# Half-height matmul pairs throughout: a spectral filter and a gated feed-forward block on one core

## The chip, the cores and the metric

The kernel runs on one core of one Trainium2 chip. The metric is the device time of one execution in microseconds. The profiles shown come from one execution that the hardware profiler recorded; their times are microseconds from the start of the span unless marked ns. PE is the matrix engine (its weight loads are PEld), DVE the vector engine, ACT the scalar engine, POOL the general engine, SP the queue that issues most DMAs.

## The reference

```python
xn = _layernorm(x, axis=-1)                       # x: 1 x 2048 x 448
y  = irfft2(rfft2(xn) * (w_r + 1j * w_i), s=(2048, 448))
gate, up = xn @ W_gate, xn @ W_up                 # 448 x 1792 each
h  = relu(gate) * up
out = x + y + h @ W_down                          # 1792 x 448
```

All in float32. The kernel works in pairs of float16 numbers, a high part and the rest, so that one product of float32 numbers becomes three float16 products: high by high, high by low, low by high.

## The kernel before, in words

The 2048 rows stand as 16 blocks `n2` of 128 rows. Four column chunks `q` hold four blocks each: 512 rows of x, transposed into `Tq[q]`, with the 448 features on the partitions. The 1792 hidden features are 14 tiles `f` of 128, in three groups of 5, 5 and 4.

**Units.** A gate-and-up unit is one tile `f` and one chunk `q`. It fills one `gu` tile of two PSUM banks, one for gate (`g` = 0) and one for up (`g` = 1); there are two such tiles. Since 448 is three times 128 and 64 more, a bank takes ten full matmuls of 128 rows by 512 columns (`SEQ`, line 905 in the profile) and one of 64 rows (`TOP`, line 912). The 64-row ones of two units are put together by `gu_halves`: four stand in a row, two for a unit and two for its mate, the next unit, which they open. Two of them, on the upper and the lower 64 rows of the array and in two banks, form a pair. A unit is then read by ACT (`gu_relu`, line 940), DVE (`gu_times`, line 944), ACT (`gu_hi`, line 948) and DVE (`gu_lo`, line 952), which leave `h` as high and low part. The `gu` tile is free after line 944.

**Down blocks.** A block of 128 rows takes `3 * len(group)` matmuls of 128 by 448 into one `dn` bank of two (`dn_mm`, line 976). ACT seeds the bank with the running sum (`dn_seed`, line 969) and takes it out again (`dn_post`, line 980). Four blocks of a chunk follow each other after the second unit at the latest that comes behind the chunk's last unit. The last four are written out by hand at the end (`dn_end`, line 1008).

**The transforms.** The spectral part runs as background work in a list `bg`, item by item, between the units. Its products are `f_dft` (line 467) and `i_ddft` (line 801), 48 half-height matmuls of 58 or 56 columns each in alternation on the two halves, `f_sdft` (line 500), three full ones of 464 columns, and `i_sdft` (line 771), twelve full ones of 128 columns, each for one block. They use two `fx` banks. Their additions and rotations are on DVE.

**Order.** An opening is written out by hand (`OPENING`); it holds the first five units. Behind it, a scheduler lays each engine's instructions in order from a time line, by priority and by what is ready; the program gives the order of units, priorities, and a few edges (`issue_after`, `add_manual_dep`). How much background work goes to a unit is set by `took`, `PE_US` and `LASTGU`, the number of units at the end that get none.

Of the kernel before, what the change touches and what calls it, by code (L numbers as in the profile page):

```python
# [10 lines left out]
F32 = mybir.dt.float32  # L11
# [6 lines left out]
S, D, F = 2048, 448, 1792  # L18
NF = F // 128
KC = 29  # L20
NG = 8
GW = 2 * KC
XW = NG * GW
# [17 lines left out]
"""  # L41
EXPMASK = 0x7F800000
EXPONE = float(1 << 23)
LASTGU = 9
SQ = 2.0 ** -16


# [99 lines left out]
def tile_gfnet_reglu(ctx: ExitStack, tc: tile.TileContext, x, xr, wgu, wd, wf, ident, c_fd, c_fm, c_im, c_row, c_id,  # L147
                     out):
    nc = tc.nc
    V, A, P, G = nc.vector, nc.scalar, nc.tensor, nc.gpsimd  # L150
# [4 lines left out]
    def mt(shape, dt, name, bufs=1):  # L155
        return main.tile(shape, dt, name=name, bufs=bufs)
# [4 lines left out]
    def fx():  # L161
        return psum.tile([128, 512], F32, name="fx", bufs=2)
# [8 lines left out]
    Tq = {q: mt([128, 9, 512], F16, f"T{q}") for q in CHUNKS}  # L171
# [11 lines left out]

    eps = mt([128, 1], F32, "eps")
    V.memset(eps, 1e-5)

# [19 lines left out]
    state = {}  # L206
# [27 lines left out]
    wst, wdst, fm_t, im_t, wf_t = {}, {}, {}, {}, {}  # L234
# [133 lines left out]
    tp, side, last = {}, {}, {}  # L368
# [40 lines left out]
        copy(Tq[q][:, (3, 4, 8)[i], :], tp["end", i], act)  # L409


    Fq, Xh, yps, cur = {}, {}, {}, {}
    RT = float(np.sqrt(0.5))

# [28 lines left out]
    def chained(m, prev):  # L443
        if "opened" in state and prev is not None:
            tc.add_manual_dep(m, prev.name, NOSYNC, reason="half passes stand together")
        return m

    def two_banks():
# [43 lines left out]
    def f_lo(a, n2):  # L492
        V.tensor_tensor(Xh[n2][:, 1], f_part(a, n2), Xh[n2][:, 0], op=OP.subtract)

    def f_sdft(n2):
        y = fx()[:, 0:XW]
        yps[n2] = y.rearrange("p (g c k) -> p g c k", g=NG, c=2)
        m, xh = fm_t[n2], Xh[n2].rearrange("p a g k -> p a (g k)")
        for i, (a, b) in enumerate(((0, 0), (0, 1), (1, 0))):
            P.matmul(y, m[:, a, :], xh[:, b], start=(i == 0), stop=(i == 2), skip_group_check=True)  # L500

    def rotate(t, b, p, sgn):

# [124 lines left out]
    sps, pg, pgh, vt = {}, {}, {}, {}  # L628
# [136 lines left out]
    def i_sdft(n2):  # L765
        ps = fx()
        v, m = state["vt"][:, :, n2 // 8].rearrange("p a g k -> p a (g k)"), im_t[n2]
        for g in range(4):
            o = ps[:, 128 * g:128 * (g + 1)]
            for i, (h, c) in enumerate(((0, 0), (0, 1), (1, 0))):  # L770
                P.matmul(o, v[:, h, 128 * g:128 * (g + 1)], m[:, c, :], start=(g + i == 0), stop=(i == 2),  # L771
                         skip_group_check=True)
        sps[n2] = ps

    def i_pqhi(n2):
        pgh[n2] = it([128, 1024], F16, "wf", 6).rearrange("p (a k) -> p a k", a=2)
# [49 lines left out]
    wt, wdt, wsc = {}, {}, {}  # L826
# [67 lines left out]
    hps, ht = {}, {}  # L894

    SEQ = [(r + 4 * k, r) for r in range(3) for k in (0, 1)] + [(t, 5 + t) for t in range(3)] + [(3, 4)]
    TOP = ((slice(0, 64), 3), (slice(64, 128), 4))

    def gu_open(f, q):
        hps[f, q] = psum.tile([128, 2, 512], F32, name="gu", bufs=2)  # L900

    def gu_full(f, q, gs, cs, start, stop, seq=SEQ):
        for g in gs:
            for i, (a, b) in enumerate(seq):
                last["P"] = P.matmul(hps[f, q][:, g, cs], wt[f, g][:, a, :], Tq[q][:, b, cs],  # L905
                                     start=(start and i == 0), stop=(stop and i == len(seq) - 1)).ins
# [8 lines left out]
    NOSYNC = mybir.DependencyInfo(mybir.DependencyClass.NoSync, mybir.DependencyReason.DATA)  # L915
    opened = set()

    def gu_unit(f, q, mate):

        gs, cs = (0, 1), slice(0, 512)  # L920
        if (f, q) in opened:
            gu_full(f, q, gs, cs, False, True)
            return
        gu_open(f, q)
        gu_full(f, q, gs, cs, True, False)
        gu_halves(f, q, mate)
# [33 lines left out]
    dps = {}  # L960
# [4 lines left out]
    def dn_seed(g, n2):  # L965

        dps[n2] = dn_bank()
        seeded.add(n2)
        A.activation(dps[n2][:, 0:D], xy[n2], AF.Copy, scale=dinv[:, g:g + 1])  # L969

    def dn_mm(fs, n2):
        q, j = n2 % 4, n2 // 4
        js = slice(128 * j, 128 * (j + 1))
        for f in fs:
            for a, b in ((0, 0), (0, 1), (1, 0)):
                last["P"] = P.matmul(dps[n2][:, 0:D], ht[f, q][:, a, js], wdt[f][:, b, :], start=False,  # L976
                                     stop=(f == fs[-1] and a == 1), skip_group_check=True).ins

    def dn_post(g, n2):
        last["A"] = A.activation(xy[n2], dps[n2][:, 0:D], AF.Copy, scale=dsc[:, g:g + 1]).ins  # L980
        seeded.discard(n2)
        if n2 in late:
            late.discard(n2)
            i_acc(n2)
# [33 lines left out]

    bg = []
    marks = {}  # L1020
    PE_US = {"f_dft": 0.85, "f_sdft": 0.59, "i_sdft": 0.65, "i_ddft": 0.82, "row_dft": 0.2}

    def add(cost, fn, *a):
        bg.append((cost, PE_US.get(fn.__name__, 0.0), fn, a))

# [37 lines left out]
    for k, a in enumerate(seq):  # L1063
        add(1.99, f_a, a)
        add(2.14, f_b, a)
        for n2 in (a, a + 8):
            add(0.0, f_hi, a, n2)
        if k:
            for n2 in (seq[k - 1], seq[k - 1] + 8):
                add(1.09 * (n2 >= 8), f_y1, n2)  # L1070
        if k < 7:
            add(0.0, f_dft, seq[k + 1], seq[k + 1] + 8)
        for n2 in (a, a + 8):
            add(0.54, f_lo, a, n2)
            add(0.0, f_sdft, n2)
        for fn, q in extra.get(k, ()):
            fn(q)
    for n2 in (7, 15):
# [8 lines left out]
    def back(k0):  # L1087
        add(bf[0], inv1, k0)
        if k0 >= 4:
# [6 lines left out]
    rows = [lambda: (row_wf(), row_hi()), row_lo, lambda: row_dft(0), row_mul, row_hi2, row_lo2,  # L1096
            lambda: row_dft(1), row_ev]
# [30 lines left out]
    def both(c, fn, p):  # L1128
        for n2 in (p, p + 8):
            add(c, fn, n2)  # L1130
# [11 lines left out]
    for p in range(8):  # L1142
        if p:
            both(0.6, i_pqlo, p - 1)
            add(0.0, i_ddft, p - 1, p + 7)
        if p < 7:
            both(0.0, load_im, p + 1)
        add(2.14, i_mix, p, 1)
        add(0.0, i_hi, p)
        if p < 6:  # L1150
            bring(p + 2)
        add(1.1, i_lo, p)
        both(0.0, i_sdft, p)
# [34 lines left out]
    groups, f0 = [], 0  # L1188
# [176 lines left out]
    for i, u in list(enumerate(units))[len(groups[0]):]:  # L1365
        is_gu = u[0] == "gu"
        if is_gu:
            _, g, f, q = u
            run_bg(until=marks["T", q])
            gu_unit(f, q, (mates.get(u) or (0, 0, None, None))[2:])  # L1370
        elif i < len(units) - 4:
            _, g, n2, _ = u
            dn_mm(groups[g], n2)
            nxt = [v for v in units[i + 1:i + 3] if v[0] == "dn"][1:]
# [8 lines left out]
        if i >= len(units) - 4:  # L1383
            continue
        if is_gu:
            with tc.high_priority(offset=400):
                gu_post(f, q)
                if units[i + 1][0] == "dn" and i + 1 < len(units) - 4:
                    for v in units[i + 1:i + 3]:
                        dn_seed(v[1], v[2])  # L1390
        else:
            with tc.high_priority(offset=400):
                dn_post(g, n2)
                for v in nxt:
                    dn_seed(g, v[2])
            if g == len(groups) - 1:
                store(n2)
        anchors.append(last["V"])
        act_anchors.append(last["A"])
    run_bg(until=len(bg))  # L1400
    dn_end(len(groups) - 1, [u[2] for u in units[-4:]])


_ORDER = ["x", "xr", "wgu", "wd", "wf", "ident", "c_fd", "c_fm", "c_im", "c_row", "c_id"]
# [42 lines left out]
```

## Time and profile before

| | |
|---|---|
| Time, median of 2 runs | 440.02 us (439.99 to 440.05) |
| The profiled execution's own time | 440.03 us |
| Its span | 438.3 us |
| PE busy | 431.6 us, 98% |
| DVE busy | 372.7 us, 85% |
| ACT busy | 255.7 us, 58% |
| POOL busy | 37.6 us, 9% |
| DMA moved | 39.53 MB, mean 90 GB/s |

The page of the profile gives busy time by engine, the groups of instructions by line of the kernel with their mean length, and the chain of work that ended last. Matmuls are pipelined: the length of one reaches past the start of the next, so the rate of PE is read from the distance between starts in the timeline. A row of the timeline merges instructions of one line: start, time to the end of the last, engine, line, count, and in brackets the idle time ahead of it with what ended it.

### The profile page before, as it was taken

To read this page: it belongs to the slowest core of one execution; us is meant where nothing else is said; L and a number is where in the kernel's file an instruction comes from. 1 tells how busy PE (TensorE), PEld (TensorE's weight loads), DVE (VectorE), ACT (ScalarE), POOL (GpSimd) and SP (SyncE) were. 2 spreads that over 40 slices of the span, in tenths; PEclk is the share of its full clock that TensorE was granted. 3 is DMA by queue.
4 is the path that set the end of the run, shared out by engine and by line. 5 is a ranking of instruction groups with operands and counts; after the bars stand their busy time and mean duration, and the time that the engine had idled before them with its cause. 6 is when DMAs were issued, how large, how long until landed. Compare 5 with 4: busy or idle time off the path is not lost.

```text
span 438.3 us, 8110 instructions
## 1 busy us (share of the span) xinstructions
PE 431.6 (98%) x3014; PEld 209.5 (48%) x3014; DVE 372.7 (85%) x920; ACT 255.7 (58%) x516; POOL 37.6 (9%) x72
## 2 busy tenths in 40 slices
PE   7999999999999999999999999999999999999997
PEld 3644544454444444444444444444555555554544
DVE  6998798999977989899999999798999989867213
ACT  6897493686457855724513675564665754763630
POOL 1140040043400040000000011000000000000000
PEclk9999999999999999999999999999999999999999
DMA  7869992042000463531402100020111211301102
GB/s 258 265 164 320 339 256 64 2 68 43 3 1 0 145 190 113 165 126 35 134 8 85 44 1 1 2 84 3 55 57 45 73 61 33 119 30 43 51 35 84
DMA packets 37720, 39.53 MB, mean 90 GB/s; under 512 B 17952, under 2 KB 32576, under 8 KB 37680
## 3 DMA queue, kind: packets, MB, share of 16 engines
q1 hardware_dynamic: 37680, 39.01, 29.6%
q8 instruction: 23, 0.38, 0.4%
q14 instruction: 17, 0.14, 0.1%
HBM read 24.25 MB, written 3.67 MB: 64 GB/s over the span
## 4 chain that ended last, share of the span: by engine, by line
PE 97%; ACT 1%; DVE 1%; DMA 1%; issue 0%
PE gu L905 56%; PE dn L976 27%; PE gu L912 3%; PE fx L771 2%; PE fx L500 2%; PE fx L467 1%; PE fx L801 1%; PE dn L1008 1%; PE gu L1008 1%; DMA y<-in_xr 1%; ACT tt L330 1%; PE fx L406 0%; DVE bst L265 0%; PE fx L1008 0%; ACT junk L192 0%
## 5 line engine op out<-in xcount | busy, mean ns | idle before, releaser
L905 PE MATMUL gu<-T,wt 128*128 128x512 f16 (+1 forms) x1138 | 256.1, 376 | 0.0
L905 PEld LDWEIGHTS <-wt 128*128 128x128 f16 x1138 | 108.1, 98 | 130.3 <-issue 10.2
L976 PE MATMUL dn<-wdt,h 128*128 128x448 f16 x624 | 126.6, 353 | 0.0
L976 PEld LDWEIGHTS <-h 128*128 128x128 f16 x624 | 60.2, 98 | 57.4 <-issue 0.7
L948 ACT ACTIVATE h<-g 128x512 f16<-128x512 f32 x56 | 35.1, 627 | 67.4 <-DVE g L944 67.2
L944 DVE SCALAR_TENSOR_TENSOR g<-gu,g 128x512 f32<-128x512 f32 x56 | 38.4, 686 | 24.0 <-ACT g L940 23.8
L940 ACT ACTIVATE g<-gu 128x512 f32<-128x512 f32 x56 | 33.0, 589 | 36.3 <-PE gu L905 18.9
L952 DVE TENSOR_TENSOR h<-g,h 128x512 f16<-128x512 f32 x56 | 38.3, 686 | 7.0 <-ACT h L948 7.0
L980 ACT ACTIVATE xy<-dn,dsc 128x448 f32<-128x448 f32 x44 | 27.6, 628 | 28.4 <-PE dn L976 28.4
L195 POOL PARTITION_ALL_REDUCE wm<-wm x15 | 14.1, 947 | 170.4 <-ACT junk L192 170.4
L969 ACT ACTIVATE dn<-xy,dinv 128x448 f32<-128x448 f32 x44 | 27.7, 632 | 0.6
L858 DVE SCALAR_TENSOR_TENSOR wt<-wst,wsc,wt 128x512 f16<-128x512 f32 x28 | 20.4, 745 | 3.4 <-ACT wt L854 3.4
L854 ACT ACTIVATE wt<-wst,wsc 128x512 f16<-128x512 f32 x28 | 19.2, 714 | 1.0 <-DVE wsc L202 0.9
L192 ACT ACTIVATE junk<-wst 128x512 bf16<-128x512 f32 x28 | 17.4, 621 | 1.8 <-DMA wst<-in_wgu 1.5
L912 PE MATMUL gu<-T,wt 64*128 64x512 f16 x112 | 17.0, 382 | 0.0
L520 DVE TENSOR_TENSOR y<-y,y 128x464 f32<-128x464 f32 x21 | 13.4, 637 | 1.1 <-DMA row<-y 1.0
L780 DVE SCALAR_TENSOR_TENSOR wf<-fx,wf 128x512 f16<-128x512 f32 x16 | 10.5, 687 | 4.4 <-ACT wf L777 4.3
L265 DVE BATCH_NORM_STATS2 bst<-y 128x6 f32<-128x448 f32 x16 | 9.2, 620 | 5.1 <-DMA y<-in_xr 5.1
L521 DVE TENSOR_TENSOR y<-y,y 128x464 f32<-128x464 f32 x21 | 13.4, 636 | 0.0
L771 PEld LDWEIGHTS <-vt 128*128 128x128 f16 x192 | 11.5, 98 | 1.9
L771 PE MATMUL fx<-im,vt 128*128 128x128 f16 x192 | 12.2, 219 | 0.0
L807 ACT ACTIVATE xy<-fx,fsc 128x448 f32<-128x448 f32 x14 | 8.1, 630 | 6.9 <-PE fx L801 6.9
(162 smaller groups left out, 500.4 us busy)
## 6 DMA issues: line engine op xcount, KB each, us to landing
wst<-in_wgu SPq DMA_DIRECT2D x28, 256.0 KB
wf<-in_wf SPq DMA_DIRECT2D x16, 232.0 KB
sw<-y SPq DMA_DIRECT2D x32, 114.2 KB
sw<-wst SPq DMA_DIRECT2D x16, 228.4 KB
y<-in_xr SPq DMA_DIRECT2D x16, 224.0 KB
xy<-in_x SPq DMA_DIRECT2D x16, 224.0 KB
out<-xy SPq DMA_DIRECT2D x15, 224.0 KB
wdst<-in_wd SPq DMA_DIRECT2D x14, 224.0 KB
```

Of the source, the lines that this page charges most:

```text
L771: P.matmul(o, v[:, h, 128 * g:128 * (g + 1)], m[:, c, :], start=(g + i == 0), stop=(i == 2), skip_group_check=True)
L854: A.activation(w[:, 0:4, :], wst[f, g], AF.Copy, scale=wsc[f, g])
L858: V.scalar_tensor_tensor(w[:, 4:8, :], st, sc, w[:, 0:4, :], op0=OP.mult, op1=OP.subtract)
L905: last["P"] = P.matmul(hps[f, q][:, g, cs], wt[f, g][:, a, :], Tq[q][:, b, cs], start=(start and i == 0), stop=(stop and i == len(seq) - 1 ...
L912: m = P.matmul(hps[f, q][:, g, 0:512], wt[f, g][rows, 7, :], Tq[q][rows, b, :], start=start, stop=not start).ins
L940: last["A"] = A.activation(g1s[f, q], hps[f, q][:, 0, :], AF.Relu, scale=2.0 ** -22).ins
L944: last["V"] = V.scalar_tensor_tensor(g1, hps[f, q][:, 1, :], 2.0 ** -22, g1, op0=OP.mult, op1=OP.mult).ins
L948: A.activation(ht[f, q][:, 0, :], g1s[f, q], AF.Copy)
L952: V.tensor_tensor(h[:, 1, :], g1s.pop((f, q)), h[:, 0, :], op=OP.subtract)
L969: A.activation(dps[n2][:, 0:D], xy[n2], AF.Copy, scale=dinv[:, g:g + 1])
L976: last["P"] = P.matmul(dps[n2][:, 0:D], ht[f, q][:, a, js], wdt[f][:, b, :], start=False, stop=(f == fs[-1] and a == 1), skip_group_check= ...
L980: last["A"] = A.activation(xy[n2], dps[n2][:, 0:D], AF.Copy, scale=dsc[:, g:g + 1]).ins
```

## The change

All gate-and-up matmuls behind the opening, all down blocks but the last four, and the products `f_sdft` and `i_sdft` become half-height matmuls, issued in pairs. In a pair, one matmul works on the upper 64 rows of the array and writes one bank, the other works on the lower 64 rows and writes another bank. A first round gives each bank one half of the rows, a second round the other half with the sides swapped. The 64-row products of a unit form one more pair of that unit; mates remain in the opening only.

A bank must not be written from both halves at once. So the first matmul of the second round waits for a memset of one element, `tick`, on POOL, and that memset waits for the last matmul of the first round.

Down blocks are now units of two blocks, which fill both `dn` banks together. At most one such unit stands between two gate-and-up units, and the first comes behind the first unit of the next chunk. `f_sdft` and `i_sdft` take two blocks, and both `fx` banks, at a time. `LASTGU` goes from 9 to 7, and the costs that spread the background work follow the new sizes.

```diff
-LASTGU = 9
+LASTGU = 7
...
+    tick = mt([1, 1], F32, "tick")
...
+    SIDE = (slice(0, 64), slice(64, 128))
...
+    def ended(m):
+        with tc.high_priority(offset=4000):
+            r = G.memset(tick, 0.0).ins
+        tc.add_manual_dep(r, m.name, SYNC, reason="behind the rows' product")
+        return r
+
+    def beside(pair, start, stop, prev=None, skip=True):
+        m = None
+        for o, w, x in pair:
+            with tc.high_priority(offset=2000 if m else 0):
+                m = chained(P.matmul(o, w, x, start=start, stop=stop, skip_group_check=skip).ins, m)
+            if prev is not None:
+                tc.add_manual_dep(m, ended(prev).name, SYNC, reason="the other half of the rows has ended")
+                prev = None
+        last["P"] = m
+        return m
...
-    def f_sdft(n2):
+    def f_sdft(a, b):
...
+        for s in range(2):
+            for i, (c, d) in enumerate(((0, 0), (0, 1), (1, 0))):
+                r = beside([(y, m[SIDE[k != s], c, :], xh[SIDE[k != s], d]) for k, (y, m, xh) in enumerate(prods)],
+                       s + i == 0, s == 1 and i == 2, r if s and i == 0 else None)
...
-    def gu_unit(f, q, mate):
...
+    def gu_unit(f, q):
+        fresh = (f, q) not in opened
+        if fresh:
+            gu_open(f, q)
+        passes = [[(*TOP[g], 7) for g in range(2)]] if fresh else []
+        passes += [[(SIDE[g != s], b, a) for g in range(2)] for s in range(2) for a, b in SEQ]
+        for i, p in enumerate(passes):
+            m = beside([(hps[f, q][:, g, :], wt[f, g][rows, a, :], Tq[q][rows, b, :]) for g, (rows, b, a) in enumerate(p)],
+                   fresh and i == 0, i == len(passes) - 1, m if i == len(passes) - 10 else None, False)
...
-    def dn_mm(fs, n2):
+    def dn_mm(fs, ns):
...
+        for s in range(2):
+            for f in fs:
+                for a, b in ((0, 0), (0, 1), (1, 0)):
+                    r = beside([(dps[n2][:, 0:D], ht[f, q][SIDE[k != s], a, js[k]], wdt[f][SIDE[k != s], b, :])
+                            for k, n2 in enumerate(ns)], False, s == 1 and f == fs[-1] and a == 1,
+                           r if s and f == fs[0] and a + b == 0 else None)
...
-        if k % 2 and pend:
-            units += pend
-            pend = []
+        if pend and pend[0][2] % 4 != u[3]:
+            units.append(pend.pop(0))
         if u[2] == groups[u[1]][-1]:
-            pend = [("dn", u[1], u[3] + 4 * j, None) for j in range(4)]
+            pend += [("dn", u[1], u[3] + 8 * j, u[3] + 8 * j + 4) for j in range(2)]
...
-    took = lambda u: 4.55 if u[0] == "gu" else 0.56 * len(groups[u[1]])
+    took = lambda u: 4.55 if u[0] == "gu" else 1.12 * len(groups[u[1]])
```

More of the change, by code (lines that the diff above doesn't have):

```diff
@@ L493, in f_lo @@
         V.tensor_tensor(Xh[n2][:, 1], f_part(a, n2), Xh[n2][:, 0], op=OP.subtract)
-    def f_sdft(n2):
[L496 to L500, printed above, removed]
+    def f_sdft(a, b):
+        prods = []
+        for n2 in (a, b):
+            y = fx()[:, 0:XW]
+            yps[n2] = y.rearrange("p (g c k) -> p g c k", g=NG, c=2)
+            prods.append((y, fm_t[n2], Xh[n2].rearrange("p a g k -> p a (g k)")))
+        for s in range(2):
+            for i, (c, d) in enumerate(((0, 0), (0, 1), (1, 0))):
+                r = beside([(y, m[SIDE[k != s], c, :], xh[SIDE[k != s], d]) for k, (y, m, xh) in enumerate(prods)],
+                       s + i == 0, s == 1 and i == 2, r if s and i == 0 else None)
     def rotate(t, b, p, sgn):
@@ L763, in i_lo, with i_sdft @@
             V.scalar_tensor_tensor(lo[:, b], u[:, b], fsc[:, 0:1], hi[:, b], op0=OP.mult, op1=OP.subtract)
[L765 to L773, printed above, removed]
+    def i_sdft(a, b):
+        prods = []
+        for n2 in (a, b):
+            sps[n2] = fx()
+            prods.append((sps[n2], state["vt"][:, :, n2 // 8].rearrange("p a g k -> p a (g k)"), im_t[n2]))
+        for s in range(2):
+            for g in range(4):
+                o = slice(128 * g, 128 * (g + 1))
+                for i, (h, c) in enumerate(((0, 0), (0, 1), (1, 0))):
+                    r = beside([(ps[:, o], v[SIDE[k != s], h, o], m[SIDE[k != s], c, :])
+                            for k, (ps, v, m) in enumerate(prods)], s + g + i == 0, s == 1 and i == 2, r if s and g + i == 0 else None)
     def i_pqhi(n2):
@@ L969, in dn_seed @@
         A.activation(dps[n2][:, 0:D], xy[n2], AF.Copy, scale=dinv[:, g:g + 1])
-    def dn_mm(fs, n2):
[L972 to L977, printed above, removed]
+    def dn_mm(fs, ns):
+        q = ns[0] % 4
+        js = [slice(128 * (n2 // 4), 128 * (n2 // 4 + 1)) for n2 in ns]
+        for s in range(2):
+            for f in fs:
[3 more added lines that the diff above has]
+                           r if s and f == fs[0] and a + b == 0 else None)
     def dn_post(g, n2):
@@ L1020, in tile_gfnet_reglu @@
     marks = {}
-    PE_US = {"f_dft": 0.85, "f_sdft": 0.59, "i_sdft": 0.65, "i_ddft": 0.82, "row_dft": 0.2}
+    PE_US = {"f_dft": 0.85, "f_sdft": 1.18, "i_sdft": 1.3, "i_ddft": 0.82, "row_dft": 0.2}
     def add(cost, fn, *a):
@@ L1074, in tile_gfnet_reglu @@
             add(0.54, f_lo, a, n2)
-            add(0.0, f_sdft, n2)
+        add(0.0, f_sdft, a, a + 8)
         for fn, q in extra.get(k, ()):
@@ L1152, in tile_gfnet_reglu @@
         add(1.1, i_lo, p)
-        both(0.0, i_sdft, p)
+        add(0.0, i_sdft, p, p + 8)
         both(0.0, i_pqhi, p)
@@ L1369, in tile_gfnet_reglu @@
             run_bg(until=marks["T", q])
[L1370 to L1374, printed above, removed]
+            gu_unit(f, q)
+        elif i < len(units) - 2:
+            _, g, *ns = u
+            dn_mm(groups[g], ns)
         with after(LAG):
@@ L1382, in tile_gfnet_reglu @@
             run_bg(amount=room(i, load[0]) if i >= RAMP else 0.0)
-        if i >= len(units) - 4:
+        if i >= len(units) - 2:
             continue
@@ L1387, in tile_gfnet_reglu @@
                 gu_post(f, q)
-                if units[i + 1][0] == "dn" and i + 1 < len(units) - 4:
-                    for v in units[i + 1:i + 3]:
-                        dn_seed(v[1], v[2])
+                if units[i + 1][0] == "dn" and i + 1 < len(units) - 2:
+                    for n2 in units[i + 1][2:]:
+                        dn_seed(units[i + 1][1], n2)
         else:
             with tc.high_priority(offset=400):
-                dn_post(g, n2)
-                for v in nxt:
-                    dn_seed(g, v[2])
+                for n2 in ns:
+                    dn_post(g, n2)
             if g == len(groups) - 1:
-                store(n2)
+                for n2 in ns:
+                    store(n2)
         anchors.append(last["V"])
@@ L1400, in tile_gfnet_reglu @@
     run_bg(until=len(bg))
-    dn_end(len(groups) - 1, [u[2] for u in units[-4:]])
+    dn_end(len(groups) - 1, [n2 for u in units[-2:] for n2 in u[2:]])
 _ORDER = ["x", "xr", "wgu", "wd", "wf", "ident", "c_fd", "c_fm", "c_im", "c_row", "c_id"]
```

8 lines of the change are left out of this document (1 added, 7 removed).

## The prediction

> **What bounds the kernel now.** I read the page's head and its groups first, then the matrix engine's waits. The execution that was profiled took 440.03 us, the median of the runs shown is 440.02 us and the span is 438.3 us, so some 1.7 us lie around the span and the sum below needs no scaling.
>
> ```profile
> span 438.3 us, 8110 instructions
> PE 431.6 (98%) x3014; PEld 209.5 (48%) x3014; DVE 372.7 (85%) x920; ACT 255.7 (58%) x516; POOL 37.6 (9%) x72
> ...
> L905 PEld LDWEIGHTS <-wt 128*128 128x128 f16 x1138 | 108.1, 98 | 130.3 <-issue 10.2
> ...
> L948 ACT ACTIVATE h<-g 128x512 f16<-128x512 f32 x56 | 35.1, 627 | 67.4 <-DVE g L944 67.2
> ...
> L980 ACT ACTIVATE xy<-dn,dsc 128x448 f32<-128x448 f32 x44 | 27.6, 628 | 28.4 <-PE dn L976 28.4
> ...
> L969 ACT ACTIVATE dn<-xy,dinv 128x448 f32<-128x448 f32 x44 | 27.7, 632 | 0.6
> ```
>
> ```profile
> PE dn L1257 <- POOL bw L1329: 1.9, 1, 1.9
> PE gu L384 <- DVE tt L357: 0.7, 2, 0.5
> ```
>
> The reader is to see that PE is busy for 98% and that its view of waits has rows of the opening alone: warming matmuls and transposes. So what PE issues is what the kernel takes. A busy PE says nothing of gaps that its modelled ends cover, so I went to the distance from start to start. The lines grouped between 43.86 and 425.69 us, behind the opening and ahead of the end:
>
> ```profile
> L905 PE MATMUL gu<-T,wt 128*128 128x512 f16 x990 | 227.2, 380 | 0.0
> L976 PE MATMUL dn<-wdt,h 128*128 128x448 f16 x624 | 126.6, 353 | 0.0
> L912 PE MATMUL gu<-T,wt 64*128 64x512 f16 x100 | 15.2, 382 | 0.0
> L771 PE MATMUL fx<-im,vt 128*128 128x128 f16 x192 | 12.2, 219 | 0.0
> ...
> L467 PE MATMUL fx<-fd_t,T 64*128 64x58 f16 x384 | 6.6, 186 | 0.0
> L801 PE MATMUL fx<-idc_t,wf 64*128 64x56 f16 x384 | 6.3, 184 | 0.0
> ```
>
> and runs of one kind in the timeline (start, us, count):
>
> ```profile
> 251.82 8.37 PE L905 MATMUL gu<-T,wt 128*128 128x512 f16 x38
> ...
> 175.78 5.46 PE L976 MATMUL dn<-wdt,h 128*128 128x448 f16 x28
> ...
> 325.22 1.39 PE L771 MATMUL fx<-im,vt 128*128 128x128 f16 x22
> ```
>
> Less the length of the last one, (8.37 - 0.38) / 37 = 216 ns from start to start at 512 columns, (5.46 - 0.35) / 27 = 189 ns at 448 and (1.39 - 0.22) / 21 = 56 ns at 128: 0.417 ns a column and 2.7 ns more. Then a place where PE goes to half-height matmuls and back, twice:
>
> ```profile
> 119.09 0.73 PE L976 MATMUL dn<-wdt,h 128*128 128x448 f16 x3
> 119.75 0.61 PE L912 MATMUL gu<-T,wt 64*128 64x512 f16 x4
> 120.29 4.49 PE L905 MATMUL gu<-T,wt 128*128 128x512 f16 x20
> 124.71 0.83 PE L467 MATMUL fx<-fd_t,T 64*128 64x58 f16 x48
> 125.47 0.74 PE L976 MATMUL dn<-wdt,h 128*128 128x448 f16 x3
> ```
>
> Three matmuls of 189 ns from 119.09 end at 119.66, but the halves start at 119.75: 0.09 us lost going in. Four halves take 0.54 us, two pairs at 216 would take 0.43: so a pair does run as one, and 0.11 is lost, most of it going out. The twenty from 120.29 take 4.42 where 20 x 216 is 4.32: 0.10, nearly all of it going in again. An excursion into half height costs **0.21 us**, and nothing else is lost behind the opening.
>
> **The change, part by part.**
>
> *Fewer changes of height.* The window has 100 / 4 = 25 excursions for gate and up, 384 / 48 = 8 in each of the two column transforms: 41. Afterwards nearly everything there is half height; full height stays in the opening, two row transforms and the last four blocks, about 3 excursions. Saved: 38 x 0.21 = **8.0 us**.
>
> *Twice the matmuls, in pairs.* A unit had 20 full ones and two pairs for two mates, thus 21 slots; it has 21 pairs now. Down blocks and the transforms of 464 and 128 columns keep their slots likewise. Is a pair a slot? At 58 columns the 48 halves take 0.83 - 0.19 = 0.64 us for 23.5 pairs, 27 ns; a full one would take 58 x 0.417 + 2.7 = 27. At 512 the first pair and the change out make 0.54 us above. So 0 us; the bounds are -2.7 ns (the fixed part hidden) and +5 ns (half of the 0.11 us, if the change out were only 0.10) on some 1900 slots: -5 to +10 us. I take 0, the value of the 58-column row.
>
> *The wait between the rounds.* The first matmul of the second round waits for a one-element memset on POOL, which waits for the last matmul of the first round. It stands in 51 units (56 by L948's count, less 5 of the opening), 22 pairs of down blocks, 8 and 8 transforms: **89 waits**. Trace rows for its steps, from the timeline and, for the memset, the lines of POOL:
>
> ```profile
> 1.30 0.53 POOL L1329 MEMSET bw<- 128x512 f16 x1
> ...
> 1.89 0.61 PE L1257 MATMUL dn<-bw 128*128 128x512 f16 x1 [1.89 <-POOL bw L1329]
> ...
> L1435 POOL MEMSET const-float32-0.0<- 128x1 f32 x1 | 0.1, 103 | 0.2 <-issue 0.2
> ...
> 164.57 0.60 PE L912 MATMUL gu<-T,wt 64*128 64x512 f16 x4
> ...
> 165.22 0.60 ACT L940 ACTIVATE g<-gu 128x512 f32<-128x512 f32 x1 [1.12 <-PE gu L912]
> ...
> 8.82 0.18 ACT L192 ACTIVATION_READ_ACCUMULATOR junk<-wst 128x1 f32 x1
> ...
> 9.10 0.40 POOL L195 PARTITION_ALL_REDUCE wm<-wm  x1 [7.27 <-ACT junk L192]
> ```
>
> PE to POOL isn't in the trace; it lies between PE to ACT (165.17 to 165.22, 0.05 us) and ACT to POOL (9.00 to 9.10, 0.10). The memset is 0.10, POOL to PE 1.83 to 1.89, 0.06. A matmul of 512 is 0.38 long, 0.22 of which is its own slot. So a bare wait idles PE for 0.16 + (0.05 to 0.10) + 0.10 + 0.06 = 0.37 to 0.42 us; I take 0.40. Behind the waiting matmul stands everything on PE, in order. Uncovered, 89 x 0.40 = **36 us**, over four times the saving.
>
> What covers it is other PE work put into the program's order there. The scheduler does so now:
>
> ```profile
> 153.33 0.37 PE L500 MATMUL fx<-Xh,fm 128*128 128x464 f16 x1
> 153.54 0.38 PE L905 MATMUL gu<-T,wt 128*128 128x512 f16 x1
> 153.75 0.36 PE L500 MATMUL fx<-Xh,fm 128*128 128x464 f16 x1
> ```
>
> One product waits for its operand's low part, and gate matmuls stand between its pieces. Two slots of 216 ns cover 0.40. Ready is the next pair of down blocks, where its banks are seeded, or the next unit, where its gate bank is free. That fails where three units stand in a row: the bank is that of the unit just ended, and the wait comes some 2.4 us behind that end. The bank can be read late:
>
> ```profile
> 181.98 0.61 PE L912 MATMUL gu<-T,wt 64*128 64x512 f16 x4
> ...
> 187.58 0.69 DVE L944 SCALAR_TENSOR_TENSOR g<-gu,g 128x512 f32<-128x512 f32 x1
> ```
>
> The unit ended at 182.59, its bank is read out at 188.27. Each of the 12 runs over a column chunk has two such places: 24. I count half of them uncovered: 12 x 0.40 = **4.8 us**. The ends are none and all 89.
>
> *POOL's queue.* A memset also waits for what POOL is at. POOL works 37.6 of 438.3 us, 9%, so 8 of 89 meet a piece of work and lose half of about 0.5 us: **2 us**. Ends: 0, and 8 us if the one long sum below (106.05) hits.
>
> ```profile
> 106.05 7.03 POOL L195 PARTITION_ALL_REDUCE wm<-wm  x2 [11.27 <-ACT junk L192]
> ```
>
> *VectorE.* From 230 to 300 us it is at 66.35 of 70:
>
> ```profile
> 230.00:300.00 70.00, 70.00 (x348) 31.94 (x346) 66.35 (x163) 39.80 (x92) 4.53 (x6) 1.00 0.11 34
> ```
>
> A PE that gains 2% leaves DVE 3% there, and the units' banks, already 5 us late, come due about 4.5 us behind a unit. I take **2 us** for a few such stalls; ends 0 and 8.
>
> *Down blocks in twos, and the rest.* A pair needs both banks evicted and seeded, 2 x (0.63 + 0.63) = 2.5 us of ACT, behind a unit of 4.5 us; ACT is at 57% in that stretch, so 0, and 0.5 us for each of 22 if it isn't. The background work ends two units later, some 9 us, while its last half matmuls now stand ahead of a tail in which PE alone counts: 0, or 2 us. The two `fx` banks are taken together by a pair of transforms: 0, the units cover it.
>
> Sum: 440.0 - 8.0 + 4.8 + 2 + 2 = **441 us**.
>
> A rule of the Trainium skill speaks against pairs. TensorE: Matmul & The Clock Gate, section "LDWEIGHTS (loading the stationary operand)": a load's time follows its columns, not its rows, about 107 ns for 128 columns, so half-height loads would cost as much as full ones. Two loads a slot, 213 ns, would pass the 189 and the 56 ns slots and add some 45 us (an estimate from that page). Two loads and two matmuls in 27 ns at 58 columns disagree; by rows it is a rival below.
>
> **The rivals.**
>
> *No cover* (slower; the other side). If the order holds nothing ready at the waits, each idles 0.37 to 0.42: 440 - 8 + 33 to 37 = 465 to 469. It decides from 20 bare waits on (8.0 / 0.40), and passes the 2% at 42. For it: PE can't pass a waiting matmul. Against: the row at 153.54. Chance 0.10.
>
> *POOL answers late.* Cover was ordered for 0.4 us and POOL takes 0.2 more each time: 89 x 0.2 = 18 us, 450, with 2 to 8 for the queue up to 458. For it, POOL's copies of one form spread threefold; against it, its memset ran 0.30 beside a busy DVE:
>
> ```profile
> L340 POOL COPY tt<-tt x12: 232/359/773, 22.6 to 93.5; 128x64 f16<-128x64 f16 x12
> ...
> 159.80 0.67 DVE L944 SCALAR_TENSOR_TENSOR g<-gu,g 128x512 f32<-128x512 f32 x1
> ...
> 160.29 0.30 POOL L666 MEMSET rowh<- 128x232 f16 x1
> ```
>
> Chance 0.14. The Trainium skill, SBUF — State Buffer, section "SBUF: two separate sides", has VectorE instructions with two inputs hold off only those of GpSimd that read: a memset would go free. These rows agree with it.
>
> *All covered.* Every wait has two slots of other work: 440 - 8 = 432 to 434. For it, PE's view of waits is empty behind the opening today, though its operands come from ACT, DVE and queues. Against, the late banks. Chance 0.20.
>
> *Loads don't overlap.* Two loads of 98 ns a pair: 196 ns hides in a slot of 216, not in 189 or 56. 624 x 7 ns + 192 x 140 ns = 31 us: 463. The 27 ns row speaks against. Chance 0.03.
>
> *The change doesn't do what it says:* pairs at 512 columns don't run side by side for long. At +10 ns a pair, 19 us more: 455 or so with the rest. Chance 0.03.
>
> **How the numbers follow.** My forecast, some waits bare, 441 us (434 to 449), has 0.50. A measurement of this kernel tells about 2% from no change: 431.2 and 448.8. Faster than 431.2 needs every wait covered and the 2.7 ns a slot as well: 0.03, out of the all-covered case. Slower: 0.10 + 0.14 + 0.03 + 0.03 and 0.03 of the forecast's upper end, 0.33. The rest, 0.64, is no change. The range reaches from all covered, 432, to the late POOL's upper end, 459; no cover, serial loads and the faster end stay out, about 0.16.
>
> **What would show it.** Right: no change of height behind the opening but at the row transforms and the end; 216 ns from pair to pair at 512 columns; 89 short memsets on POOL about 0.5 us behind a matmul's start; matmuls of another bank between two rounds; idle PE of some 9 us that POOL and DVE end. Idle PE over 20 us with POOL as the releaser shows a rival. Wrong it would be by a pair's pitch away from 216, or by a PE that waits for DVE over long stretches.

## The result and the profile after

The changed kernel takes **533.9 us** (533.8 to 534.0), the kernel before 440.0: a ratio of 1.213, 95% interval 1.211 to 1.215. The execution that was profiled took 534.0 us, its span is 532.2. From the page, the busy times, the row of the granted clock in 40 slices and the chain that ended last:

```profile
span 532.2 us, 12061 instructions
PE 465.8 (88%) x4898; PEld 257.0 (48%) x4898; DVE 378.8 (71%) x920; ACT 251.9 (47%) x516; POOL 38.6 (7%) x161
...
PEclk9999678978999989998999999799997998978999
...
PE 45%; DVE 29%; ACT 15%; DMA 5%; issue 4%; SPq 1%; POOL 0%; ACTq 0%; DVEq 0%; POOLq 0%
```

DVE, ACT and POOL do the work they did before (372.7, 255.7 and 37.6 us then). PE was busy for 98% and is now at 88% of a span 94 us longer, and the chain leaves PE for more than half of the time. PE's waits (us in total, times, longest), which were rows of the opening alone:

```profile
PE gu L464 <- DVE g L976: 14.4, 10, 3.7
PE dn L464 <- ACT dn L1001: 11.5, 9, 3.7
PE dn L464 <- ACT h L980: 10.0, 3, 5.0
PE fx L464 <- ACT xy L838: 6.1, 4, 5.4
PE fx L464 <- ACT eo L495: 5.9, 2, 5.4
PE dn L464 <- DVE h L984: 2.9, 4, 1.2
...
PE gu L464 <- POOL tick L455: 1.5, 1, 1.5
```

L464 is the line of every paired matmul now; L976 is `gu_times`, which frees the unit's banks, L1001 `dn_seed`, L980 and L984 leave `h`, L838 and L495 empty the `fx` banks. So PE stops for ACT and DVE, up to 5.4 us at a time, and hardly for the new memset, though there are 89 of it:

```profile
L455 POOL MEMSET tick<- 1x1 f32 x89 | 8.1, 91 | 361.2 <-PE gu L464 146.6
```

Are the pairs slow themselves? Runs of one kind in the timeline say no:

```profile
249.78 1.46 PE L464 MATMUL gu<-T,wt 64*128 64x512 f16 x12
251.07 3.00 PE L464 MATMUL dn<-wdt,h 64*128 64x448 f16 x30
253.91 2.75 PE L464 MATMUL gu<-T,wt 64*128 64x512 f16 x24
```

Twelve pairs from 253.91 to 256.66: (2.75 - 0.38) / 11 = 215 ns from pair to pair. Fifteen pairs of down blocks from 251.07 to the next row's start: 2.84 / 15 = 189 ns.

I followed one half of the rows by itself (every second one of the half-height matmuls, and all full ones), from start to start, behind 41 us. On it, 2121 of 2365 steps lie within 15 ns of 0.417 ns a column and 2.7 more. The other 244 lose 102 us together; before, all steps lost 8. Of the 102, 44 us are at matmuls that waited for ACT last, 25 for DVE, 4 for POOL. In the remaining 29 no wait is recorded. Some 24 of them lie in stretches at a granted clock of 0.5 behind a stop, and 19 of these at 126 steps that show just the slower pace (at 512 columns 0.43 us apart instead of 0.22). The others are in part at halves whose partner was held up.

One stop, from the timeline of all engines (start, us; in brackets the idle time ahead and what ended it):

```profile
463.71 0.59 PE L464 MATMUL gu<-T,wt 64*128 64x512 f16 x3
464.09 0.57 ACT L972 ACTIVATE g<-gu 128x512 f32<-128x512 f32 x1
464.22 1.31 DVE L791 SCALAR_TENSOR_TENSOR vt<-wst,fsc,vt 128x464 f16<-128x464 f32 x2 [1.17 <-ACT vt L786]
...
467.23 0.63 DVE L422 TENSOR_TENSOR wst<-wst 128x464 f32<-128x464 f32 x1
467.78 0.68 DVE L976 SCALAR_TENSOR_TENSOR g<-gu,g 128x512 f32<-128x512 f32 x1
...
468.50 0.63 ACT L980 ACTIVATE h<-g 128x512 f16<-128x512 f32 x1 [3.84 <-DVE g L976]
...
469.03 1.14 ACT L838 ACTIVATE xy<-fx,fsc 128x448 f32<-128x448 f32 x2
...
469.70 0.26 PE L464 MATMUL fx<-im,vt 64*128 64x128 f16 x1 [5.40 <-ACT xy L838]
```

PE's next matmul needs an `fx` bank that L838 empties. L838 stands in ACT's order behind L980, L980 needs L976, and L976 stands in DVE's order behind background work: its input was ready at 464.66, when L972 ended, and DVE came to it at 467.78. ACT was idle for 3.84 us with L838 behind it. Over the whole span DVE is busy for 71% and ACT for 47%; here the orders of three engines didn't fit each other.

### The profile page after: what moved, and what is told of

It is laid out like the page before. It is cut to its first block, busy times and chain, and to the rows that moved or that the text cites. A ratio compares the mean times of both kernels' runs of the same rounds, so it can differ in the third digit from the quotient of the medians.

```text
span 532.2 us, 12061 instructions
## 1 busy us (share of the span) xinstructions
PE 465.8 (88%) x4898; PEld 257.0 (48%) x4898; DVE 378.8 (71%) x920; ACT 251.9 (47%) x516; POOL 38.6 (7%) x161
## 4 chain that ended last, share of the span: by engine, by line
PE 45%; DVE 29%; ACT 15%; DMA 5%; issue 4%; SPq 1%; POOL 0%; ACTq 0%; DVEq 0%; POOLq 0%
PE gu L464 26%; PE dn L464 14%; PE fx L464 3%; DVE g L976 3%; ACT junk L193 2%; DMA xy<-in_x 2%; ACT xy L1015 2%; ACT dn L1001 2%; DMA y<-in_xr 2%; DVE h L984 1%; ACT g L972 1%; DVE wf L811 1%; DVE vt L791 1%; DVE y L549 1%; DVE tt L363 1%
## 5 line engine op out<-in xcount | busy, mean ns | idle before, releaser
L464 PE MATMUL gu<-T,wt 64*128 64x512 f16 x2140 | 273.1, 394 | 15.9 <-DVE g L976 14.4
L464 PEld LDWEIGHTS <-wt 64*128 64x128 f16 x2140 | 131.1, 98 | 126.8 <-issue 36.2
L464 PE MATMUL dn<-wdt,h 64*128 64x448 f16 x1248 | 153.3, 357 | 25.1 <-ACT dn L1001 11.5
L464 PEld LDWEIGHTS <-h 64*128 64x128 f16 x1248 | 76.7, 95 | 82.8 <-issue 19.4
L976 DVE SCALAR_TENSOR_TENSOR g<-gu,g 128x512 f32<-128x512 f32 x56 | 38.5, 688 | 66.6 <-ACT g L972 66.3
L972 ACT ACTIVATE g<-gu 128x512 f32<-128x512 f32 x56 | 33.1, 590 | 90.4 <-PE gu L464 90.4
L980 ACT ACTIVATE h<-g 128x512 f16<-128x512 f32 x56 | 35.0, 625 | 56.6 <-DVE g L976 56.5
L984 DVE TENSOR_TENSOR h<-g,h 128x512 f16<-128x512 f32 x56 | 38.4, 687 | 11.4 <-ACT h L980 11.4
L464 PE MATMUL fx<-Xh,fm 64*128 64x464 f16 x96 | 18.3, 397 | 9.1 <-ACT eo L495 5.9
L1001 ACT ACTIVATE dn<-xy,dinv 128x448 f32<-128x448 f32 x44 | 26.2, 631 | 0.0
L464 PE MATMUL fx<-im,vt 64*128 64x128 f16 x384 | 15.8, 226 | 8.8 <-ACT xy L838 6.1
L936 PE MATMUL gu<-T,wt 128*128 128x512 f16 (+1 forms) x118 | 22.4, 347 | 0.0
L464 PEld LDWEIGHTS <-vt 64*128 64x128 f16 x384 | 13.8, 99 | 13.8 <-issue 7.7
L513 ACT ACTIVATE Xh<-eo 128x464 f16<-128x464 f32 x16 | 9.2, 598 | 20.5 <-DVE eo L443 20.5
L516 DVE TENSOR_TENSOR Xh<-eo,Xh 128x464 f16<-128x464 f32 x16 | 9.9, 638 | 11.3 <-ACT Xh L513 11.3
```

What stands on the lines that cost most here:

```text
L464: m = chained(P.matmul(o, w, x, start=start, stop=stop, skip_group_check=skip).ins, m)
L972: last["A"] = A.activation(g1s[f, q], hps[f, q][:, 0, :], AF.Relu, scale=2.0 ** -22).ins
L976: last["V"] = V.scalar_tensor_tensor(g1, hps[f, q][:, 1, :], 2.0 ** -22, g1, op0=OP.mult, op1=OP.mult).ins
L980: A.activation(ht[f, q][:, 0, :], g1s[f, q], AF.Copy)
L984: V.tensor_tensor(h[:, 1, :], g1s.pop((f, q)), h[:, 0, :], op=OP.subtract)
```

## The experiments

Theories. **ORDER**: the waits made the scheduler put in later units' matmuls, whose inputs come late. **HALVES**: the order was laid by a time line in which a pair is longer than a slot of the chip, so it is wrong with the waits or without. **UNITS**: down blocks in twos starve PE. From the fifth run on the rival is **PITCH**: half-height pairs cost on the chip by themselves, and no order mends it. Each time below is that of one execution, the last run's the median of four; the kernel before took 439.9 to 440.4 us beside them.

**Pairs without swap and waits.** Both rounds on the same sides:

```diff
-        passes += [[(SIDE[g != s], b, a) for g in range(2)] for s in range(2) for a, b in SEQ]
+        passes += [[(SIDE[g], b, a) for g in range(2)] for s in range(2) for a, b in SEQ]
...
-                   fresh and i == 0, i == len(passes) - 1, m if i == len(passes) - 10 else None, False)
+                   fresh and i == 0, i == len(passes) - 1, None, False)
```

and so in `dn_mm`, `f_sdft` and `i_sdft`. Each product leaves out half of its rows and takes the other half twice, so the output is not the reference's; the count of matmuls is the same.

> The second round works on the same half of the rows as the first, so no bank is written from both halves and the 89 waits for POOL go; each product is computed from one half of its rows, twice, at the same count of matmuls. Theory ORDER (the waits make the scheduler fill PE's order with matmuls of later units, whose inputs from ACT and DVE come later on the chip than in its time line): without waits 432 to 440 us, PE's stops on ACT and DVE gone. Theory HALVES (the scheduler's time line has a wrong length for pairs of halves, so that its order is wrong with or without waits): 500 to 534 us, the same stops. Theory UNITS (down blocks in twos starve banks): 500 us or more.

Measured: 483.2 us. Without a wait for POOL 43 us more than before are left, and they are the same sort of stop:

```profile
PE fx L490 <- ACT eo L495: 7.9, 1, 7.9
PE gu L464 <- DVE g L976: 7.0, 3, 4.1
```

That lies between the 432 to 440 of ORDER and the 500 to 534 of HALVES: the waits aren't the whole cause, and not none of it.

**Full height with the waits.** The same units, slots and 89 waits; round `s` fills bank `s` with full-height matmuls:

```diff
-        passes += [[(SIDE[g != s], b, a) for g in range(2)] for s in range(2) for a, b in SEQ]
+        passes += [[(slice(0, 128), b, a)] for s in range(2) for a, b in SEQ]
```

> The changed kernel's units, waits and counts of slots, but each slot is one full-height matmul: the first round fills the first bank, the second round the second, with the same 89 waits between; only the 64-row pair of each unit stays half height. Theory ORDER: 500 to 545 us, PE stops on ACT and DVE as in the changed kernel. Theory HALVES: 440 plus 26 more excursions at 0.21 us (5 us) plus what of the waits is bare, 445 to 460 us. Theory UNITS: 500 us or more.

Measured: 473.9 us, 34 above the kernel before with no pair but the 64-row one of each unit; ORDER gave 500 to 545, HALVES 445 to 460, and neither holds. Full height without the waits takes 449.9 us (below), so waits and the order laid for them come to about 24 at full height. (That kernel also issues a group's products in another order, so the 24 aren't the waits alone.)

**Units in order.** The first matmul of each unit behind the last of the unit before, on PE:

```diff
+            u = last.get("U") if i == 0 else None
...
-                   fresh and i == 0, i == len(passes) - 1, m if i == len(passes) - 10 else None, False)
+                   fresh and i == 0, i == len(passes) - 1, m if i == len(passes) - 10 else None, False, u)
+        last["U"] = m
```

> The changed kernel with one edge more for each unit: its first matmul stands behind the last one of the unit before on PE, so only background products can stand in a wait. Theory ORDER: the waits are bare (73 of them at 0.40 us, 29 us), but PE's stops on ACT and DVE go: 440 - 8 + 29 = 461, up to 475 us, faster than the changed kernel though its waits are uncovered. Theory HALVES: 515 us or more. Theory UNITS: 515 us or more.

Measured: 547.7 us, so this expectation failed. The run is of use for the price of a wait. A bare one and a long one, in the timelines of PE and POOL:

```profile
229.67 2.32 PE L464 MATMUL gu<-T,wt 64*128 64x512 f16 x20
...
232.13 0.09 POOL L455 MEMSET tick<- 1x1 f32 x1 [5.57 <-PE gu L464]
...
232.27 2.33 PE L464 MATMUL gu<-T,wt 64*128 64x512 f16 x20 [0.28 <-POOL tick L455]
```

```profile
108.62 0.28 POOL L340 COPY tt<-tt 128x56 f16<-128x56 f16 x1 [12.12 <-ACT tt L349]
...
112.53 0.09 POOL L455 MEMSET tick<- 1x1 f32 x1
...
112.67 1.89 PE L464 MATMUL gu<-T,wt 64*128 64x512 f16 x8 [11.03 <-POOL tick L455]
```

Ten pairs from 229.67 should take 2.16; the second round starts 2.60 later: **0.44 us** bare. The memset starts 0.13 to 0.14 us behind the end of the last matmul (231.99). Of 71 waits 55 lie between 0.430 and 0.440, taken from the half that is held up less. The long one isn't a slow POOL: the memset stands in POOL's order behind copies, the first of which waited 12 us for ACT.

**Down blocks in twos alone.** The kernel before with the new units, their cost and `LASTGU`:

```diff
-            pend = [("dn", u[1], u[3] + 4 * j, None) for j in range(4)]
+            pend += [("dn", u[1], u[3] + 8 * j, u[3] + 8 * j + 4) for j in range(2)]
```

> The kernel before with nothing but the down blocks in twos between units, their cost and the 7 units at the end without background work; all matmuls as before, no waits. Theories ORDER and HALVES: 437 to 444 us. Theory UNITS: 500 us or more, PE waiting for seeds of the down banks.

Measured: 440.2 us; UNITS falls.

**Full height, no waits, in the changed kernel's slots, and its order given to the pairs.** The first of these two kernels issues a full-height matmul for each pair's slot. The second builds it, reads off the order of every engine, and builds the pairs (no swap, no waits, so half of each product's rows is left out again) behind edges that hold this order. In the full-height one a group begins with one product of the second bank, then come those of the first and the rest of the second; what reads either bank waits for both.

```diff
+    MODE.update(full=False, swap=False, wait=False, order={e: order[e] for e in order if e.split(".")[-1] in ('PE', 'DVE', 'Activation', 'SP', 'Pool')})
+    nc, made = build()
...
+                for m in by.get((e, k), []):
+                    if prev is not None:
+                        tc.add_manual_dep(m, prev.name, NOSYNC, reason="a given order")
+                    prev = m
```

> The changed kernel's units, slots and order of issue, but each slot a full-height matmul (bank 0 first, then bank 1) and no waits. Only the single 64-row pair of each unit stays half height, so there are some 51 + 16 excursions at 0.21 us where the kernel before has 41. Every theory: 440 + 26 x 0.21 = about 445 us, 440 to 452. If it comes out above 465, it is the grouping of two banks to one unit (both banks released at one time) that costs, not pairs or waits.

> Pairs of half-height matmuls without the swap and without the waits, as in the run without both, so each product is taken from one half of its rows twice; but the order of instructions on every engine behind the opening is pinned to the one that the full-height kernel without waits has. HALVES (the schedule was laid by a time line in which a pair takes longer than a slot, so matmuls, ACT and DVE work stand in a bad order): the 43 us are gone, full-height time less 60 excursions x 0.21 = 12 us, so 430 to 438 us. PITCH (pairs on the chip are slower or release their banks later in a way that order can't mend): 470 to 485 us, like the run without pinning.

Measured: 449.9 and **444.8 us**. The same pairs that took 483.2 in the order laid for them take 444.8 in the order laid for full height. In the second:

```profile
PE gu L468 <- DVE g L1004: 5.6, 4, 2.1
```

L1004 is `gu_times` here; this is the largest wait behind the opening. Of full height's 449.9, some 5 us are 26 more excursions (134 changes of height, 82 before, at 0.10) and 5 are stops for DVE and ACT. The pairs save 12.5 of changes and come out only 5.1 lower, so 7 are lost to more stops; hence 444.8 and not the 430 to 438 that HALVES gave. PITCH falls: it gave 470 to 485.

**One engine's order or two.** The same pairs with PE's order alone pinned, and with DVE's and ACT's alone:

```diff
-    ... order={e: order[e] for e in order if e.split(".")[-1] in ('PE', 'DVE', 'Activation', 'SP', 'Pool')})
+    ... order={e: order[e] for e in order if e.split(".")[-1] in ('PE',)})
```

> As the pinned run without swap and waits (each product from one half of its rows twice), but only the matrix engine's order is pinned to the full-height one; VectorE, ScalarE, GpSimd and the DMA queues keep the order that the schedule of the pairs lays. If the order on PE is what costs, 430 to 440 us. If it is the order on VectorE and ScalarE (releases standing behind background work), 455 to 485 us. I lean to something between, 445 to 460.

> Pairs without swap and waits (each product from one half of its rows twice), with only VectorE's and ScalarE's order pinned to the full-height one; the matrix engine keeps the order that the schedule of pairs lays. The complement of the run with PE alone pinned (471.7), between 483.2 with nothing and 444.8 with all pinned. If the order on DVE and ACT is the greater part: 448 to 460 us. If either order alone spoils it: 465 to 483.

Measured: 471.7 and 482.7 us. PE's order alone gives 11.5 of the 38.4 us back, DVE's and ACT's alone 0.5; all of it comes only with every engine's order pinned, those of POOL and SP too. My lean to 445 to 460 and the first figure for the second run (448 to 460) were wrong.

**The change whole, in an order laid for full height with waits**, and **the reverse**, full height with waits in the changed kernel's own order. Both by the edges above.

> The changed kernel whole (pairs, swap, 89 waits), with the order on every engine behind the opening pinned to that of the full-height kernel with the same 89 waits, which took 473.9 us. HALVES: 474 less some 10 us of changes of height, 460 to 468 us, so about 70 of the 94 us are the order and the rest are waits. PITCH: no better than 520. If the waits in the swap cost by themselves more than at full height (a pair of banks must drain together): 480 to 500.

> The reverse: full-height matmuls, one for each pair's slot, with the 89 waits, but the order on every engine behind the opening pinned to the one that the changed kernel has. With its own order this computation took 473.9 us. HALVES (the order that is laid for pairs is what costs): as slow as the changed kernel, 533.9, plus some 5 to 10 us of changes of height less what the single pairs' neighbours hide, 520 to 545 us. PITCH (half-height pairs themselves cost on the chip): close to 474, below 490.

Measured: **479.7** and **555.4 us**. The change gains 54 us of its 94 back by another order alone. It misses the 460 to 468 of HALVES and comes out at the lower end of the third case (480 to 500: the waits in the swap cost more than at full height). Its largest waits are

```profile
PE dn L468 <- ACT dn L1029: 11.2, 15, 3.6
PE fx L468 <- ACT Xh L546: 4.3, 1, 4.3
PE fx L468 <- POOL tick L457: 3.9, 11, 0.7
```

L1029 is `dn_seed`. A pair needs both banks seeded at its first matmul. From start to start on one half this run loses 47.6 us where the 444.8-us run loses 12.5: 7 at waits for POOL, 31 at waits for ACT and DVE (partners held up counted) and 8 at the low clock. (The order was laid for the full-height program whose groups begin with one product of the second bank; in this it differs from the 473.9-us kernel, and it wasn't timed.) In the reverse, full-height matmuls in the changed kernel's order are slower than the pairs were, and have their stops:

```profile
PE gu L468 <- POOL tick L457: 14.0, 47, 1.3
PE dn L468 <- ACT dn L1027: 13.0, 9, 3.4
PE gu L468 <- DVE g L1002: 10.4, 9, 3.2
```

That is above the 520 to 545 expected, and part of it is this run's own. Since a group begins with one product of the second bank, its wait stands one slot later than in the pairs, and the work that covered it there no longer stands in it: 88 waits for POOL lose 40 us, 4 in the changed kernel. Without these 36 it would take some 520 us (an estimate from the two traces), still some 45 above the 473.9 of the order laid for full height with waits; 43 us are lost at waits for ACT and 13 for DVE.

**All waits bare, in the good order.** The change whole, in the order of the 444.8-us run, in which nothing was put into a wait; each memset has its own element:

```diff
-    tick = mt([1, 1], F32, "tick")
+    tick = mt([1, 89], F16, "tick")
...
-            r = G.memset(tick, 0.0).ins
+            r = G.memset(tick[:, n:n + 1], 0.0).ins
```

> The changed kernel whole (pairs, swap, 89 waits), with the order on every engine behind the opening pinned to that of the full-height kernel without waits, in which the pairs alone took 444.8 us. That order puts nothing on purpose into a wait; each wait has a one-element memset of its own element. BARE WAITS (a wait costs its own round trip and nothing else): 444.8 + 89 x 0.44 = 484 us, less what other work happens to stand there, 470 to 486, nearly all of PE's idle time with POOL as its end. QUEUE (memsets stand in POOL's order behind work that waits for ACT and DVE, as in the run with units in order): 500 or more, with single waits of several us.

Measured: 510.0 us, 65 above the same order without swap and waits, and now POOL ends PE's stops:

```profile
PE gu L469 <- POOL tick L458: 22.9, 50, 7.4
PE dn L469 <- POOL tick L458: 16.8, 20, 5.2
PE fx L469 <- POOL tick L458: 4.3, 15, 1.1
```

PE's view of waits has no stop for ACT or DVE behind the opening any more. From start to start 86 waits lose 58 us (the half held up less) and the slow clock behind the long ones 11. Of the 86, 73 lose 0.37 to 0.38 us each, 27 together: a bare wait is 0.06 shorter than in the run with units in order, because the memset starts 0.07 us behind the last matmul instead of 0.13 (medians). Here it has its own element, in float16; which of the two does it, no run separates.

```profile
246.80 0.81 PE L469 MATMUL gu<-T,wt 64*128 64x512 f16 x5
...
247.67 0.09 POOL L458 MEMSET tick<- 1x1 f16 x1 [3.77 <-PE gu L469]
...
247.82 0.39 PE L469 MATMUL gu<-T,wt 64*128 64x512 f16 x2 [0.21 <-POOL tick L458]
```

Nine waits of 1.3 to 7.5 us lose 29. In each, POOL was at other work until just before the memset: some 26 us are POOL's queue, as in the longest:

```profile
57.82 0.75 POOL L342 COPY tt<-tt 128x56 f16<-128x56 f16 x1 [6.44 <-ACT tt L351]
...
63.36 0.09 POOL L458 MEMSET tick<- 1x1 f16 x1
...
63.51 1.03 PE L469 MATMUL gu<-T,wt 64*128 64x512 f16 x4 [7.37 <-POOL tick L458]
```

BARE WAITS gave 470 to 486, QUEUE 500 or more: it is QUEUE's time, with a bare wait in nearly every place and the queue in nine.

**Fewer excursions without pairs.** The runs suggest one cheaper way to the first saving: in the kernel before, move 10 of the 16 column transforms on PE to stand right behind the next four 64-row matmuls.

```diff
+            if j is not None and sum(len(r[1]) for r in runs[i + 1:j]) <= REACH and not any(
+                    k in MODE["fx"] for r in runs[i + 1:j] for k in r[1]):
+                runs.insert(j, runs.pop(i))
```

> The kernel before, full height, no waits; only the order on PE is changed behind the opening: 10 of the 16 column transforms (48 half-height matmuls each) are moved later, to stand right behind the next four 64-row gate and up matmuls, so that one excursion into half height serves both. At 0.21 us an excursion: 440.0 - 10 x 0.21 = 437.9 us. If the later transforms make background work late: 440 or more. Under 2% in either case.

Measured: 447.2 us, ratio 1.017 (1.015 to 1.019). The changes of height fall from 82 to 62, 2 us as worked out, but a transform that comes later is read later, and PE waits for that:

```profile
PE fx L504 <- ACT eo L476: 5.3, 3, 3.0
```

Here ten displaced items cost more than the ten excursions that they saved. No version beat the kernel before.

**The sum of the 94 us**, in a chain of runs: 440.0 to 444.8 (pairs, regrouped, in an order laid for full height: +5), to 479.7 (swap and waits, in an order laid for waits: +35), to 533.9 (the order laid for the pairs: +54). That the order costs the 54 is shown: the same instructions take 479.7 us in another order, and full-height ones are slow in this one too, waits at POOL taken off. The 35 are swap, waits and the order laid for them together (in the order laid without waits, swap and waits come to 65). That the order was laid by a time line too slow for pairs is argued: pairs and full height have equal slots on the chip, and only what the scheduler made of them differs. No trace shows its time line.

## Why the prediction was wrong, step by step

The step that failed is the price of cover, with the two terms that hang on it: the sum lets the scheduler fill the waits at no cost, and gives VectorE 2 us and the down blocks 0. In their place the changed kernel loses 69 us at waits for ACT and DVE and 19 at the low clock behind them, and 54 of its 94 us go with another order of the same instructions.

- *Fewer changes of height*, 8.0 us: right in kind, 7.3 in size. Five changes are left behind 41 us, 0.5 us at 0.10 each, against 82 and 7.8.
- *Pairs take one slot*, 0 us: right, 215 and 189 ns. "Loads don't overlap" and "pairs don't run side by side" fall with it, and so does what the prediction drew from the Trainium skill's page TensorE: Matmul & The Clock Gate, section "LDWEIGHTS (loading the stationary operand)". The page gives the time of one load, about 107 ns for 128 columns, and in the changed kernel a load took 95 to 99 ns by the means of its groups. But two loads and two matmuls of 448 columns go in 189 ns, less than the 213 that two such loads one after another would take.
- *A bare wait*, 0.37 to 0.42: 0.43 to 0.44 with the one element that all memsets of the change share, 0.37 to 0.38 where each has its own. The term that was low is PE to POOL: 0.13 with the shared element, 0.07 with its own, where the prediction had 0.05 to 0.10.
- *Cover*, 12 of 89 bare: the count was even too high. Five waits for POOL lose 4 us in the changed kernel. So the rival *all covered* nearly had its condition, and its 432 to 434 us didn't come. What failed is the sentence under it: "What covers it is other PE work put into the program's order there". I priced a covered wait at nothing. Cover means matmuls of other units ahead of their place, and these need banks freed and seeded earlier: as the traces suggest, the wait that was bought off on POOL came back on ACT and DVE (7 and 31 us in the 479.7-us run). Covered, swap and waits cost 35 us (479.7 against 444.8); bare, 65. My 7 us for cover and queue were a fifth of the smaller.
- *POOL's queue*, 0 to 8 us: I counted time in which POOL works. What holds a memset up is, above all, time in which POOL waits with other work at its head; where waits are bare, the queue takes 26 us.
- *VectorE*, 2 us with ends 0 and 8, and *down blocks in twos*, 0: the terms that were mis-sized. Stops for DVE and ACT are 25 and 44 us. In the 444.8-us run, with the better order and no waits, all losses from start to start are 12.5 us, nearly all of them such stops and halves held up by them: even there they are above the 8 that I gave VectorE. I worked out how busy the engines are over long stretches; what decided was whether the item PE needs stands early enough in their order. UNITS as such cost nothing (440.2).
- What the sum had no term for: that the same scheduler, given pairs, lays another order on every engine, and a worse one, with the waits (54 us) and without them (483.2 against 444.8). I took the order's tightness before, 0.4 us lost outside changes of height, as a trait of the kernel. It was a trait of that one order.
- *POOL answers late*: not borne out. The 89 memsets took 0.09 us each (median; the longest 0.13). The row at 160.29 didn't test the rule beside it either: that VectorE instruction reads `gu`, in PSUM, so it has one input in SBUF and not two.
- *No cover*, 465 to 469, the rival on the slower side: its mechanism is real, but with all waits bare the kernel takes 510, for the queue and for the clock, which falls behind long stops. In "what would show it", "a PE that waits for DVE over long stretches" is what the profile shows, with ACT beside it.

## What to carry to other kernels

Where a scheduler lays the order, a change to the kind of instruction can change the order on all engines; price that first, by giving the new instructions the old order and the old instructions the new one. A wait is not free because other work stands in it: ask which banks that work needs and who frees them. And judge an engine off the critical path by what stands ahead of the one needed item in its queue, not by its share of busy time.

## What the runs showed of the hardware

Behind a stop of some us PE runs at a granted clock of 0.5 for a while. Two stretches of the changed kernel (length; busy us of PE, PEld, DVE, ACT, POOL with counts; the clock follows):

```profile
58.50:72.20 13.70, 11.00 (x87) 4.35 (x84) 12.86 (x38) 4.26 (x9) 5.48 (x14) 0.50 0.63 141
109.70:116.60 6.90, 5.46 (x27) 2.16 (x28) 5.43 (x16) 1.53 (x3) 0.69 (x5) 0.51 0.83 154
```

They are at 0.50 and 0.51 throughout; in the same two stretches the kernel before was at 1.00. In the changed kernel 11 of the 12 stops of over 2 us end in, or within about 2 us of, such a stretch of 3.4 to 13.7 us; the twelfth (2.6 us) doesn't. So a stop costs more than its length: some 19 us in all beside 73 us of stops. A tenth of a microsecond is lost at each change of height, in either direction (at full height without waits, 12.9 us at the 130 that no stop blurs). PE to POOL to PE through a one-element memset takes 0.44 us beyond the slots where all memsets write one element, 0.38 where each writes its own.
